# Decay attention with a gated MLP on one core: softmax divided behind the value product by reciprocals sent through DRAM, the convolution off TensorE, decays of two pairs on it, and a new order

## The chip, the cores and the metric

One core of one Trainium2 chip. The metric is device time of one execution in microseconds (us). Times of the kernel before: 525.26 us, the median of 3 runs (524.59 to 526.09).

## The reference

```
scores = q @ k^T / sqrt(D)                      # q, k, v: (8, 8, 576, 64), f: (8, 8, 576)
cum    = cumsum(log(clip(f, 1e-4, 1)))
scores = where(j > i, -1e9, scores + cum[i] - cum[j])
attn   = exp(scores - max(scores));  attn = attn / (sum(attn) + 1e-9)
x      = (attn @ v) as (8, 576, 512)            # heads side by side
gate   = sigmoid(sum over k < 5 of conv_w[k] * x[s - 4 + k])    # by channel, causal
out    = (gate * (x @ w_val)) @ w_out
```

## The kernel before

The 64 heads go two at a time: 32 pairs, four pairs to a batch. A pair's 64 + 64 channels fill the 128 partitions. Its queries go in four blocks of 128 (block j against 128(j+1) keys, causal) for each head, and the last 64 queries of both heads together, 128 rows against all 576 keys: nine score blocks a pair, in three groups u = 0, 1, 2 (`SG`). For each pair:

- `load_pair`, `load_rest`: SP loads q and k (`Xr`), v (`vt`), and by broadcast reads from the DRAM tensor `decd` the decays of its two heads (`dm`, 640 KB each, `dl`, 144 KB each); POOL masks the diagonal (`affine_select`, L317).
- `plan_t`, `plan_s`: products in PSUM (`banks`), for pairs 0 to 3 in f32, then in three f32r products of high and low parts. DVE adds the decays and takes the row's minimum of the negated scores (`red`, L465), ACT takes the exponential with its sum (`ex`, L469; `P`, `Pl`, sums in `zs`). `rec` (L478, L479) adds 1e-9 and takes reciprocals, in two halves of a pair. `norm` (`times`, L276 on ACT, L278 on POOL and DVE) multiplies each exponential block by its column of `rz`.
- `plan_pt`: TensorE (PE) transposes the normalized blocks (L510, L528, L529), ACT or DVE copies them to SBUF (`pt`).
- `plan_pv`: value products in two halves of queries, copied to `x32` (`X`, ACT or DVE, L271). The convolution over x is one first tap and four multiply-adds on DVE (`cv`, L612); for pairs 0 and 1 (`NCV = 2`) it is five matmuls a half on PE against diagonal matrices. ACT takes the tanh (sigmoid in disguise, `half_tanh`, L586), with its table set loaded at pair 0.
- `plan_moe`: for each batch, x @ w_val (`Mv`), gated on DVE (`H`), and the product with w_out (`Mo`), all as three f32r products.

Pair 0's decays are not read from DRAM: PE adds them as products of a selecting matrix `pick` with the table `st` in SBUF (`SD`, `decays`), ahead of the score products, in the same banks. The weights arrive as 64-bit numbers and are decoded on ACT, DVE and POOL in the first 100 us (`decode`).

The order of the work is written out: `TABLE` is a list of steps, each with its engine and PSUM bank, and `Plan.order` records the instructions in it. Each engine runs its own in that order and waits where it must. SP issues all loads, in order too. The helper `mm` (L256) records the matmuls, `copy` (L271) the copies, `load` (L283) the DMAs.

Of the kernel before, what the change touches and what calls it, by code (L numbers as in the profile page):

```python
# [7 lines left out]
F32 = mybir.dt.float32  # L8
# [17 lines left out]
NCV = 2  # L26
# [7 lines left out]
XZ, XK4, XK, XW = 512, 640, 704, 1216  # L34
XP = ((0, XK4), (XK4, XW))
# [17 lines left out]
6y18A27Z28b2af36A19f26M028x28y18h38s078i36B18R48e18c18d38k018-
3a348o058l18t28p16C3ai38q038r28m018z19j29l28g12329k19g1aj3ad39h294073545v29929m16N0952a549i19q29y39x3by19a16J006K09b29618n26L29729c16D18u058v12416E2aD
06aE26O2bp49v19818D019w18B048C1ak00352bw3bx38E2aF1bn49d29u39r1au0149G076P1dq46U066F26G29z39H1ae36R07bz3al2am18H1az2ap2aq1252an29A00aA19B26Q36S09t1ao19
I056V09s39E009J17003710av2aB2bj4bt39K05ar2aw1ax26T2ay19F1bv3as1bT006W28I2at29M0276X16Y2aJ3aC16Z06aG2bU2aM35w18X4bl4aP39P19O29Q29N19L17229C04dw46-
0aI16H2ds4bV1aU02aV18J28K29D1aL1dy4dE3dH1bu39R079S1aK1bA052306_2bB2dF1bH2bK014bF2aO1bC1eO4bL2732bG19T06bR2bI19U1aN3aY07bS1bP2bQ1aZ28L2aH3a-
03a_1bD2b0065b42b317d00b216I1aQ07bM1eG4bN2dI27803790eX3eY3dG3aS05bE1bO1du4e001aR1bJ2bX1b12ab4bZ2c807e12g04c91eV17506eM4aW04aT1b-
37437607a2aX1e21c407dD3g24dT0542729V1c517728F2dJ02613262br47b1bW2dC3dU2eI4283d-
2c22c01b707dQ2dR19X1dK2b503dL1fW4dW28G3c31ce02dM2fY4dO2dP17c37e0dY2dZ1bY3b62c12dN1c603b81b_37i06cc079Y2eK49Z2b91dS2bb17f19W27g47j0eW2c71d_1e52cf1cd17n  # L60
019-
2ha4dX19_2ba2e41e72cg074cj2eU37o0ch2dV17k1ca00ck1e32e93eb3bc2ci28M1fg02fh2bd2gb1cb1be2fi1ef05hi4e62cn07eS37p1g91cl03e81eZ02401cm17q4dA4eT3co2cp2f7063c
r3eg1ea3e-
2f22hg4f31e_1gc3ed05f02f42fe2f11fa2ho3a017s07eh00f51ee2ei1cq37l47t07u1el02cA04fb1ec2ej01cB0hr1ek1f82ff1g63cs2cx05cy0bf2f62em1bg1ep023cC2ct2er1cI04fm1f
# [115 lines left out]
def tile_decay_attention_gated_mlp(  # L180
# [224 lines left out]
    def plan_s(i):  # L405
# [7 lines left out]
        for u, group in enumerate(SG):  # L413
# [59 lines left out]
            if u == 1:  # L473
                continue
# [337 lines left out]
```

## Time and profile before

| | us |
|---|---|
| median of 3 runs | 525.26 |
| the profiled execution | 527.36 |
| its span | 525.6 |
| PE busy (4412 matmuls) | 510.6, 97% |
| DVE busy | 450.2, 86% |
| ACT busy | 410.1, 78% |
| POOL busy | 292.1, 56% |
| DMA (16 engines) busy, mean | 54.0% of the span, 94.62 MB |

Busy time counts an engine's instructions, not what they wait for. PE's matmuls are pipelined, so their durations overlap: what one step costs is read from the start of one to the start of the next. The span is the profiled execution's own program; a sum of changes is made against its 527.36 us.

### The profile page before, as it was taken

How to read it: one execution, taken by the hardware profiler on the slowest of the kernel's cores; microseconds unless marked ns; L12 is line 12 of the kernel's file. 1: busy time of each engine (PE TensorE's matmuls, PEld its weight loads, DVE VectorE, ACT ScalarE, POOL GpSimd, SP SyncE). 2: the span in 40 equal slices, each digit the busy share in tenths (PEclk: the TensorE clock that was granted, in tenths of full speed). 3: DMA queues.
4: the chain of work that ended last, by engine and by line, in shares of the span. 5: the costliest groups of instructions: out<-in, count | busy, mean ns of one | idle time of the engine just before them, and what ended most of it. 6: DMA issues, size and time to landing. Idle time of an engine off the chain costs nothing.

```text
span 525.6 us, 12791 instructions
## 1 busy us (share of the span) xinstructions
PE 510.6 (97%) x4412; PEld 448.0 (85%) x4412; DVE 450.2 (86%) x1257; ACT 410.1 (78%) x1121; POOL 292.1 (56%) x408
## 2 busy tenths in 40 slices
PE   6899999999999999999999999999999999999997
PEld 4567779988999889998899888899899988898995
DVE  6998999989879888998988998988899998866771
ACT  4999999988868897777979978899988777464221
POOL 3636679674666674667795748653645554324100
PEclk9999999999999999999999999999999999999999
DMA  7988675656265736546736556666577271500012
GB/s 257 305 292 289 216 217 196 183 166 238 87 233 179 256 123 221 181 155 250 245 134 211 195 185 226 215 214 192 183 217 225 78 236 69 186 27 1 21 60 101
DMA packets 29905, 95.44 MB, mean 182 GB/s; under 512 B 3920, under 2 KB 3920, under 8 KB 29840
## 3 DMA queue, kind: packets, MB, share of 16 engines
q1 hardware_dynamic: 29840, 94.62, 54.0%
q8 instruction: 35, 0.57, 0.5%
q14 instruction: 30, 0.25, 0.1%
HBM read 84.69 MB, written 9.91 MB: 180 GB/s over the span
## 4 chain that ended last, share of the span: by engine, by line
PE 79%; ACT 9%; DVE 5%; DMA 3%; issue 2%; SPq 1%; POOL 0%; DVEq 0%; ACTq 0%
PE banks L256 64%; PE banks L510 12%; ACT P L469 3%; PE banks L528 2%; DMA Xr<-in_x_dram 2%; DVE banks L465 2%; ACT P L276 1%; ACT pt L271 1%; DMA dm<-decd 1%; SPq L283 1%; DMA Pl<-in_f_dram 1%; PE banks L529 1%; ACT Xh L271 0%; ACT gate L701 0%; ACT x L271 0%
## 5 line engine op out<-in xcount | busy, mean ns | idle before, releaser
L469 ACT ACTIVATE P<-banks,negm 128x128 f32<-128x128 f32 (+3 forms) x256 | 134.2, 535 | 22.0 <-DVE negm L465 20.7
L278 POOL TENSOR_SCALAR P<-P,rz 128x128 f32<-128x128 f32 (+3 forms) x113 | 77.4, 691 | 98.0 <-DVE rz L479 69.4
L465 DVE CUSTOM_DVE_ANT_0 banks<-banks,dm 128x128 f32<-128x128 f32 (+3 forms) x256 | 120.0, 513 | 11.5 <-PE banks L256 4.5
L256 PE MATMUL banks<-xh,wall 128*128 128x288 f32 x512 | 120.2, 306 | 0.0
L612 DVE SCALAR_TENSOR_TENSOR gate<-x,cw,gate 128x576 f32<-128x576 f32 x120 | 104.9, 879 | 1.3
L510 PE MATMUL banks<-ident,P 128*128 128x128 f32 x640 | 99.2, 276 | 4.2 <-ACT P L276 1.2
L271 ACT COPY pt<-banks 128x512 f32<-128x512 f32 (+2 forms) x206 | 84.5, 444 | 22.4 <-PE banks L510 10.7
L256 PE MATMUL banks<-pt,vt 128*64 128x128 f32 (+2 forms) x1408 | 95.6, 290 | 0.3 <-DVE pt L271 0.3
L256 PE MATMUL banks<-wall,hh 128*128 128x512 f32 x288 | 93.3, 405 | 0.0
L256 PEld LDWEIGHTS banks<-pt,vt 128*64 128x64 f32 x1408 | 83.6, 137 | 11.2 <-issue 2.4
L510 PEld LDWEIGHTS banks<-ident,P 128*128 128x128 f32 x640 | 75.4, 140 | 16.5 <-POOL P L278 1.8
L256 PEld LDWEIGHTS banks<-xh,wall 128*128 128x128 f32 x512 | 86.3, 188 | 0.7
L256 PE MATMUL banks<-xl,wall 128*128 128x288 f32 x256 | 75.4, 294 | 0.0
L317 POOL TENSOR_SCALAR_AFFINE_SELECT dm<-dm 128x256 f32<-128x256 f32 x126 | 56.7, 475 | 29.4 <-DMA dm<-decd 21.8
L271 DVE COPY pt<-banks 128x512 f32<-128x512 f32 (+2 forms) x114 | 49.3, 450 | 17.1 <-PE banks L510 10.4
L276 ACT ACTIVATE P<-P,rz 128x256 f32<-128x256 f32 (+3 forms) x100 | 58.2, 597 | 5.9 <-DVE rz L479 5.8
L256 PE MATMUL banks<-Xh 128*128 128x288 f32 (+4 forms) x280 | 57.6, 340 | 0.4 <-ACT P L469 0.4
L256 PEld LDWEIGHTS banks<-wall,hh 128*128 128x128 f32 x288 | 50.2, 189 | 7.7 <-ACT P L469 0.2
L256 PE MATMUL banks<-wall,hl 128*128 128x512 f32 x144 | 56.7, 394 | 0.0
L469 ACT ACTIVATION_READ_ACCUMULATOR P<-banks,negm 128x1 f32 x256 | 53.5, 209 | 0.0
L256 PE MATMUL banks<-Xh,Xl 128*128 128x288 f32 (+4 forms) x280 | 52.9, 313 | 0.0
L256 PE MATMUL banks<-Xl,Xh 128*128 128x288 f32 (+4 forms) x280 | 52.9, 313 | 0.0
(109 smaller groups left out, 875.3 us busy)
## 6 DMA issues: line engine op xcount, KB each, us to landing
dm<-decd SPq DMA_DIRECT2D x62, 640.0 KB, 5.3
Xr<-in_x_dram SPq DMA_DIRECT2D x32, 608.0 KB, 5.6
vt<-in_v_dram SPq DMA_DIRECT2D x32, 320.0 KB, 4.9
out_dram<-ot SPq DMA_DIRECT2D x36, 256.0 KB, 3.3
dl<-decd SPq DMA_DIRECT2D x62, 144.0 KB, 4.7
ot<-in_w_val_dram SPq DMA_DIRECT2D x2, 512.0 KB, 5.4
wu<-in_w_val_dram SPq DMA_DIRECT2D x2, 512.0 KB, 6.2
ot<-in_w_out_dram SPq DMA_DIRECT2D x2, 512.0 KB, 5.0
```

Of the source, the lines that this page charges most:

```text
L256: nc.tensor.matmul(out, lhsT=lhsT, rhs=rhs, start=start, stop=stop)
L271: (eng.copy if eng is nc.scalar else eng.tensor_copy)(out=out, in_=in_)
L276: eng.activation(out=out, in_=in_, func=AF.Copy, scale=col)
L278: eng.tensor_scalar(out=out, in0=in_, scalar1=col, scalar2=0.0, op0=ALU.mult, op1=ALU.add)
L283: lambda e: (nc.sync if e == "SP" else nc.scalar).dma_start(out=out, in_=in_), reads, writes, **kw)
L317: nc.gpsimd.affine_select(out=t, in_=t, pattern=[[0, 2], [-1, P]], base=0, channel_multiplier=1, compare_op=ALU.is_ge, fill=-BIG)
L465: nc.vector.tensor_tensor_reduce(out=sl, in0=sl, in1=add[:, o:o + ext], op0=ALU.add, op1=ALU.min, scale=-0.125, scalar=3.0e38, accum_out=n ...
L469: nc.scalar.activation(out=dst[:, o:o + ext], in_=bank(key)[:, c0:c0 + ext], func=AF.Exp, bias=negm[r][:, col], scale=-1.0, accum_out=zs[r ...
L510: nc.tensor.transpose(out=bank(key)[:, c:c + P], in_=Pt[m][:, BOFF[b] + P * j:BOFF[b] + P * j + P], identity=ident)
L528: nc.tensor.transpose(out=bank(key)[:, P * j:P * j + P], in_=Pl[r][:, D + P * j:D + P * j + P], identity=ident)
L529: nc.tensor.transpose(out=bank(key4)[0:D, 0:P], in_=Pl[r][:, 0:D], identity=ident)
L612: eng.scalar_tensor_tensor(out=gt, in0=src, scalar=wt_, in1=gt, op0=ALU.mult, op1=ALU.add)
```

## The change

- The exponentials go to PE undivided. The reciprocals of a pair's nine sums are computed at once, into nine extra columns of `Pl`, and transposed with its last piece, so that they come out as nine rows; a copy brings them to `rt`, two DMAs write them to the DRAM tensor `rzd`, and two DMAs read them back, each row broadcast to 64 partitions, into the pair's `x32`. The copy of a value product to `x32` becomes a multiplication by what lies there, on DVE alone. `x32` has three buffers (`NXR`).
- `NCV = 0`: the convolutions of pairs 0 and 1 go to DVE like the others.
- `ND = 2`: decays of pairs 0 and 1 are added by PE, in groups u = 0 and 2 behind the score products, in u = 1 ahead of them. Their loads from `decd` fall away.
- The tanh's table set, which has the exponential too, is loaded behind the logarithm at the start. Other keys' order in `Xr`, other buffers for the start's scratch.
- A new `TABLE`, for other costs of the steps.

```diff
-NCV = 2
+NCV = 0
+ND = 2
+NXR = 3
...
 TABLE = """
-0040b20x30930240C40a20E10430520c20y30F20s010H20G20d10e20630t000I10J20f20N40K20Y40g20L20j20M20k20l20740h10i10P10Q20S20R20T10u000U20W10r003k42940m43a42d
...
+0240040430s010w000c20u040e20f10740g10v030b30F40t010Q40520h20H10i20932g001240k12i00K20n20l10m10z32r0570C33342e30j10o43540I20J20E32h00q40630L10B32n22o12
...
-    Pl = tiles(NQ, [P, S], F32, "Pl")
+    Pl = tiles(NQ, [P, S + NN], F32, "Pl")
...
+    rt = tiles(NQ, [D + NN, P], F32, "rt")
+    rzd = dram.tile([NP, 2, S], F32, name="rzd")
...
-        for h in range(2 if i else 0):
+        for h in range(2 if i >= ND else 0):
             m = (2 * i + h) % NH
...
+    act("st0", 1.3, z, lambda: nc.scalar.preload_act_table_set(EXP_TANH), [("ln",)], [("act",)])
...
+            added = {}
+            if deep and u != 1:
+                for q, pair in enumerate(pairs if u == 0 else ((0,),)):
...
+                    pe("SD", e * 4 / 2400.0 + 0.03, p + 0.004 + 0.002 * q, lambda pair=pair, decays=decays: decays(pair, False),
...
+        def rec():
+            rz = Pl[r][:, S:]
+            nc.vector.tensor_scalar(out=rz, in0=zs[r], scalar1=1e-9, scalar2=None, op0=ALU.add)
+            nc.vector.reciprocal(out=rz, in_=rz)
...
-            def norm(eng, sl=sl, c=4 * u + n):
-                times(eng, sl, sl, rz[r][:, c:c + 1])
...
+            nc.tensor.transpose(out=bank(key4)[0:D + NN, 0:P], in_=Pl[r][:, L0:], identity=ident)
...
+        any_("PE", {"ACT": 0.16, "DVE": 0.21}, p + 0.02, lambda eng: copy(eng, rt[r][D:], bank(key4)[D:D + NN, 0:P]), [key4], [("rt", r)])
+        load("rzw", 0.1, p + 0.03, rzd[i, :, 0:L0].rearrange("h (j q) -> h j q", q=P), rt[r][D:D + 2 * NB], [("rt", r)], [("rzd", i, 0)])
+        load("rzw", 0.1, p + 0.03, rzd[i, :, L0:], rt[r][D + 2 * NB:], [("rt", r)], [("rzd", i, 1)])
+        for h in range(2):
+            load("rzr", 0.65, p + 0.04, x32[i % NXR][D * h:D * h + D, T0:], rzd[i, h:h + 1].to_broadcast([D, S]),
+                 [("rzd", i, 0), ("rzd", i, 1)], [("xb", i % NXR, h)])
...
-            def ev(eng, key=key, qa=qa, qb=qb):
-                copy(eng, xr[:, T0 + qa:T0 + qb], bank(key)[:, 0:qb - qa])
-            any_("X", ap(qb - qa), p, ev, [key], [("x", r, half)])
+            def ev(key=key, qa=qa, qb=qb):
+                o = xr[:, T0 + qa:T0 + qb]
+                nc.vector.tensor_tensor(out=o, in0=bank(key)[:, 0:qb - qa], in1=o, op=ALU.mult)
+            dve("X", (qb - qa) / 960.0 + 0.075, p, ev, [key, ("xb", rx, 0), ("xb", rx, 1)], [("x", rx, half)])
```

Three places of the order, before and now. First, PE in the start: `gate0,dm0` are the decays of pair 0, `Xr0` its products, `ident` alone the products that keep PE going, `P0` the transposition of a block of P. Before (two decays of 512 stand just ahead):

```order
L256 MATMUL banks_125<-gate0_109,dm0_68 128x256 x2
L256 MATMUL banks_125<-Xr0_73 128x512 x2
L256 MATMUL banks_125<-Xr0_73 128x256 x2
L256 MATMUL banks_125<-gate0_109,dm0_68 128x384 x2
L256 MATMUL banks_125<-Xr0_73 128x384 x2
L256 MATMUL banks_125<-gate0_109,dm0_68 128x128 x2
L256 MATMUL banks_125<-Xr0_73 128x128 x2
L256 MATMUL banks_125<-gate0_109,dm0_68 128x288
L256 MATMUL banks_125<-Xr0_73 128x288
L256 MATMUL banks_125<-gate0_109,dm0_68 128x288
L256 MATMUL banks_125<-Xr0_73 128x288
L510 MATMUL banks_125<-ident_64,P0_79 128x128 x2
```

Now:

```order
L371 MATMUL banks_126<-ident_64 128x128 x20
L253 MATMUL banks_126<-Xr0_73 128x512 x2
L253 MATMUL banks_126<-Xr0_73 128x256 x2
L253 MATMUL banks_126<-gate0_111,dm0_68 128x256 x2
L253 MATMUL banks_126<-gate0_111,dm0_68 128x384 x2
L253 MATMUL banks_126<-Xr0_73 128x384 x2
L253 MATMUL banks_126<-gate0_111,dm0_68 128x128 x2
L253 MATMUL banks_126<-Xr0_73 128x128 x2
L253 MATMUL banks_126<-gate0_111,dm0_68 128x512 x2
L511 MATMUL banks_126<-ident_64,P0_79 128x128 x2
L253 MATMUL banks_126<-Xr0_73 128x288 x2
L253 MATMUL banks_126<-gate0_111,dm0_68 128x288 x2
```

The first products of Xr stand ahead of the decays and a first transposition ahead of the last 64 queries (the rows of 288).

Second, SP in the middle of the program: before, a stretch of loads, and now the loads about pair 11 (`rt1`, `x322`) and pair 12 (`rt0`). Before:

```order
L283 DMA dm0_68<-decd_67 128x1280
L283 DMA Xr0_73<-in_x_dram 128x1216
L283 DMA dm2_70<-decd_67 128x1280
L283 DMA dm1_69<-decd_67 128x1280
L283 DMA out_0_dram<-ot_121 128x512
L283 DMA Xr1_74<-in_x_dram 128x1216
L283 DMA dl1_72<-decd_67 64x576
L283 DMA out_0_dram<-ot_121 128x512
```

Now:

```order
L280 DMA dm1_69<-decd_67 128x1280
L280 DMA x321_94<-rzd_98 64x576
L280 DMA rzd_98<-rt0_96 2x4x128
L280 DMA rzd_98<-rt0_96 2x1x64
L280 DMA x322_95<-rzd_98 64x576 x2
L280 DMA dm2_70<-decd_67 128x1280
L280 DMA Xr0_73<-in_x_dram 128x1216
L280 DMA dm1_69<-decd_67 128x1280
L280 DMA dm0_68<-decd_67 128x1280
L280 DMA vt1_88<-in_v_dram 128x640
L280 DMA rzd_98<-rt1_97 2x4x128
L280 DMA dm2_70<-decd_67 128x1280
```

Of pair 11 the two reads follow on the two writes they wait for, with the loads of later pairs behind them; of pair 12 three other loads stand between its two writes.

Third, the evacuation of a value product. Before, on ACT, two copies of one pair (`x320`) among the others:

```order
L271 COPY pt2_86<-banks_125 128x512
L271 COPY pt0_84<-banks_125 128x256
L271 COPY x320_95<-banks_125 128x384
L271 COPY x320_95<-banks_125 128x192
L276 ACTIVATE gate0_109<-x320_95,cw_66 128x576
L271 COPY pt0_84<-banks_125 128x512
L469 ACTIVATE Pl0_82,zs0_91<-banks_125,negm0_89 128x576
```

Now, on DVE, pair 11 (`x322`). Ahead of this piece stand the copy of pair 11 to `rt1` and an `xl`; the rows of L479 with a bank are row minima of later pairs:

```order
L479 ISA banks_126,negm0_89<-banks_126,dm1_69 128x512
L479 ISA negm0_89 128x1
L268 CAST xh4_103<-x321_94 128x576
L616 SCALAR_TENSOR_TENSOR gate0_111<-x321_94,cw_66,gate0_111 128x576 x2
L479 ISA banks_126,negm1_90<-banks_126,dl1_72 128x576
L479 ISA negm1_90 128x1
L490 TENSOR_SCALAR Pl0_82<-zs0_91 128x9
L491 RECIPROCAL Pl0_82<-Pl0_82 128x9
L587 TENSOR_TENSOR xl4_109<-x321_94,xh4_103 128x576
L268 COPY pt0_84<-banks_126 128x512
L580 TENSOR_TENSOR x322_95<-banks_126,x322_95 128x384
L580 TENSOR_TENSOR x322_95<-banks_126,x322_95 128x192
```

The two multiplications wait for the reads into `x322`; behind them come the gate's first tap, the next pair's copy to `rt0`, and further minima.

## Rows read from the trace of the kernel before

**Rows 1.** Busy time of each engine in six stretches of the span: start:end, length, then busy us and (instructions) of PE, its weight loads, DVE, ACT and POOL, the granted share of TensorE's clock, the DMA engines' mean busy share and GB/s.

```profile
0.00:17.59 17.59, 12.33 (x56) 8.29 (x56) 13.21 (x43) 9.72 (x23) 5.97 (x24) 1.00 0.75 242
17.59:80.00 62.41, 57.85 (x471) 44.11 (x471) 58.44 (x172) 60.62 (x169) 40.38 (x59) 1.00 0.78 263
80.00:200.00 120.00, 119.36 (x1087) 107.60 (x1086) 105.98 (x296) 103.23 (x283) 81.03 (x104) 1.00 0.57 190
200.00:320.00 120.00, 119.77 (x1091) 107.69 (x1089) 109.03 (x312) 99.31 (x280) 80.63 (x105) 1.00 0.58 196
320.00:440.00 120.00, 119.35 (x1094) 107.24 (x1095) 107.22 (x310) 102.67 (x285) 65.86 (x99) 1.00 0.60 194
440.00:525.60 85.60, 81.89 (x618) 73.08 (x616) 56.30 (x130) 34.50 (x86) 18.21 (x20) 1.00 0.18 61
```

**Rows 2.** TensorE's timeline, 31 to 34 us (start, busy us, instructions of one form merged, idle time before in brackets): the convolution of one half of pair 0 and what follows it.

```profile
31.13 0.65 PE L256 MATMUL banks<-x,h 128*128 128x288 f32 x2
...
33.56 0.65 PE L528 MATMUL banks<-ident,Pl 128*128 128x128 f32 x4
```

**Rows 3.** TensorE's timeline from the first decays to the first transposition of P, and one later piece of the same products for pair 2.

```profile
7.76 2.93 PE L256 MATMUL banks<-gate,dm 64*128 64x512 f32 x8 [1.41 <-DVE gate L361]
10.48 2.07 PE L256 MATMUL banks<-Xr 64*128 64x512 f32 x8
12.39 0.81 PE L256 MATMUL banks<-gate,dm 64*128 64x384 f32 x4
13.03 0.81 PE L256 MATMUL banks<-Xr 64*128 64x384 f32 x4
13.68 0.38 PE L256 MATMUL banks<-gate,dm 64*128 64x128 f32 x4
13.90 0.39 PE L256 MATMUL banks<-Xr 64*128 64x128 f32 x4
14.21 0.75 PE L256 MATMUL banks<-gate,dm 128*128 128x288 f32 x2
14.80 0.65 PE L256 MATMUL banks<-Xr 128*128 128x288 f32 x2
15.29 0.65 PE L256 MATMUL banks<-gate,dm 128*128 128x288 f32 x2
15.77 0.65 PE L256 MATMUL banks<-Xr 128*128 128x288 f32 x2
17.59 0.44 PE L510 MATMUL banks<-ident,P 128*128 128x128 f32 x2 [1.17 <-ACT P L276]
...
34.25 1.56 PE L256 MATMUL banks<-Xr 64*128 64x512 f32 x8
```

**Rows 4.** The timeline of all engines in the start: two DMA issues, TensorE's wait for Xr, the first cuts of the table on ACT, the first full reciprocal; and, from the view of the tile Xr in the first 20 us, its loads' time to landing.

```profile
2.04 0.58 SPq L283 DMA_DIRECT2D u<-in_conv_w_dram  x1
...
3.61 0.43 SPq L283 DMA_DIRECT2D Xr<-in_x_dram  x1
...
7.22 1.01 ACT L359 ACTIVATE gate<-x,ref 128x256 f32<-128x256 f32 x2 [1.43 <-DVE ref L352]
...
10.34 0.51 PEld L256 LDWEIGHTS banks<-Xr 64*128 64x128 f32 x4 [0.38 <-DMA Xr<-in_x_dram]
...
16.39 0.18 DVE L479 RECIPROCAL rz<-rz 128x4 f32<-128x4 f32 x1
...
DMA to landing us min/median/max: 4.8/6.2/6.7
```

**Rows 5.** Who made TensorE wait: waiter, releaser, us in total, times, longest.

```profile
PE banks L256 <- ACT P L469: 1.3, 3, 0.6
PE banks L510 <- ACT P L276: 1.2, 1, 1.2
PE banks L510 <- DVE P L278: 1.1, 2, 0.6
PE banks L510 <- POOL P L278: 0.7, 2, 0.5
PE banks L256 <- ACT gate L586: 0.7, 1, 0.7
```

**Rows 6.** DMA issues of the whole span (count, KB each, median us from issue to landing), and SP's issue of two dl loads in its timeline.

```profile
dl<-decd SPq DMA_DIRECT2D x62, 144.0 KB, 4.7
decd<-gate SPq DMA_DIRECT2D x1, 116.0 KB, 3.5
u<-in_conv_w_dram SPq DMA_DIRECT2D x1, 20.0 KB, 2.4
...
12.29 1.10 SPq L283 DMA_DIRECT2D dl<-decd  x2
```

**Rows 7.** Groups of instructions by line and form (count, busy us in all, mean ns of one, idle time before): the multiply-add of the gate, a row minimum, an xl, all on DVE; then the normalization on POOL and on ACT, from the page.

```profile
L612 DVE SCALAR_TENSOR_TENSOR gate<-x,cw,gate 128x576 f32<-128x576 f32 x120 | 104.9, 879 | 1.3
L465 DVE CUSTOM_DVE_ANT_0 banks<-banks,dm 128x512 f32<-128x512 f32 x64 | 45.2, 715 | 1.6 <-PE banks L256 1.6
L579 DVE TENSOR_TENSOR xl<-x,xh 128x576 fp32r<-128x576 f32 x13 | 9.8, 755 | 0.0
...
L278 POOL TENSOR_SCALAR P<-P,rz 128x128 f32<-128x128 f32 (+3 forms) x113 | 77.4, 691 | 98.0 <-DVE rz L479 69.4
L276 ACT ACTIVATE P<-P,rz 128x256 f32<-128x256 f32 (+3 forms) x100 | 58.2, 597 | 5.9 <-DVE rz L479 5.8
```

More of the change, by code (lines that the diff above doesn't have):

```diff
@@ L291, in tile_decay_attention_gated_mlp @@
     st = gate[0].rearrange("p g s -> p (g s)")[:, 0:SW + S]
[L292 to L294 removed]
+    ft, cum, ones = Pl[1][:, 0:S], x32[1][:, T0:], vt[1].rearrange("p a h d -> p (a h d)")[:, 0:S]
+    pick = [dm[2 * n][:, 0:2 * P] for n in range(ND)]
+    kf, kc, ko = [("Pl", 1)], [("xb", 1, 0), ("xb", 1, 1)], [("vt", 1)]
     kst = [("gate", 0, g) for g in range(G)]
@@ L381, in tile_decay_attention_gated_mlp @@
     pool("start", 0.8, z + 0.3, mk_tri, (), [("tri",)])
-    for r in range(NQ):
+    for r in range(NXR):
         pool("start", 0.1, z + 0.4 + r, lambda r=r: nc.gpsimd.memset(x32[r][:, 0:T0], 0.0), (), [("xpad", r)])
@@ L420, in plan_s, with decays, go @@
             pairs = ((0, 1), (2, 3))
-            def decays(group=group, keys=keys, pairs=pairs):
-                for n in [n for pair in pairs for n in pair]:
+            deep = i < ND
+            def decays(pair, start, group=group, keys=keys, u=u):
+                if u == 2:
+                    for a, e in ((0, 288), (288, 576)):
+                        mm(bank(keys[0])[:, 224 + a:224 + e], pick[i][:, P:], st[:, SW + a:SW + e], False, True)
+                    return
+                for n in pair:
                     h, j, c0 = group[n]
                     hs = slice(D * h, D * h + D)
-                    mm(bank(keys[n])[:, c0:c0 + EXT[j]], pick[hs, 0:P], st[hs, BOFF[j]:BOFF[j] + EXT[j]], True, False)
-            if i == 0 and u == 0:
-                pe("SD", 2.0, p - 0.15, decays, [("dm", 0), *ktab[:2], *kst], list(dict.fromkeys(keys.values())),
-                   cols=3072, mode=1)
-            def go(group=group, keys=keys, u=u, pairs=pairs, decays=decays):
+                    mm(bank(keys[n])[:, c0:c0 + EXT[j]], pick[i][hs, 0:P], st[hs, BOFF[j]:BOFF[j] + EXT[j]], start, not start)
+            def go(group=group, keys=keys, u=u, decays=decays):
                 if u == 2:
@@ L743, in tile_decay_attention_gated_mlp, with scores @@
     plan_w("wo", w_out, woh, wol, 3.6)
-    for i in range(NP):
+    def scores(i):
         if i:
@@ L749, in tile_decay_attention_gated_mlp @@
         plan_s(i)
+    for i in range(NP):
+        if i == 0 or i >= ND:
+            scores(i)
         plan_pt(i)
+        for n in range(1, ND if i == 0 else 0):
+            scores(n)
         plan_pv(i)
```

283 lines of the change are left out of this document (131 added, 152 removed).

## Prediction

> **What bounds the kernel now.** I read the busy time by stretch first, then TensorE's timeline, then its waits. In the busy times by stretch [rows 1] the reader is to see TensorE (PE) at 358.5 of the 360 us between 80 and 440 us, while DVE stands at 322.2, ACT at 305.2 and POOL at 227.5 there. What PE does not fill lies at the ends: 5.3 us idle before 17.59, 4.6 us from there to 80, and 3.7 us in the last stretch, behind the last product. So from 80 us on, work taken from PE comes off the time and work taken from another engine does not. From 17.59 to 80 all three are close: ACT 60.6, DVE 58.4, PE 57.9 of 62.4. The granted clock is 1.00 in every stretch, so no term is a clock term. The profiled execution took 527.36 us; the median of the runs is 525.26, 2.1 lower. I make the sum against the first and carry it to the second.
>
> **The convolution leaves PE.** A half's ten matmul instructions start at 31.13, and the next step's start at 33.56 [rows 2]: 2.43 us. Two pairs by two halves are 4 x 2.43 = 9.7 us of PE gone. The eight multiply-adds that replace them go to DVE at 879 ns each [rows 7], 7.0 us. Behind 80 us that is free, since DVE has 37.8 us idle in 360. Ahead of 80 us DVE has 4.0 idle in all, but the gates of pairs 0 and 1 are not wanted before the first batch's value product. I cost it at nothing, and take up the other case below.
>
> **Decays of pair 1 on PE.** Pair 1 now pays what pair 0 paid. The blocks of 384 take 0.64 us (12.39 to 13.03), those of 128 0.22 (13.68 to 13.90), the last 64 queries 0.59 and 0.48 (14.21 to 14.80, 15.29 to 15.77) [rows 3]. Those of 512 and 256 lie between 1.56 us, which the same shapes of Xr take at 34.25, and 2.72, which they took at 7.76 with a wait in it; I take 1.5, near the unstalled row. Together 3.4 us (to 4.6). **PE's work: -9.7 + 3.4 = -6.3 us** (-5.1 to -6.5). Its transposes, value products and projections stay as they are.
>
> **The start.** Before, PE waits for the first cut of the decays (7.76), then for Xr (10.34), and the first transposition starts at 17.59, when ACT has divided a block by a reciprocal of 16.39 [rows 3, 4]. In the new order the first products need no decays, Xr is issued where conv_w was, at 2.04 and not 3.61, and the transposition needs only the exponential. Xr's loads take 4.8 to 6.7 us to land, so products start between 6.8 and 8.7. The tables come off ACT from 7.22 on at about 0.5 us each, ahead of their use. Then PE has 1.56 us of products (as at 34.25), 1.5 of their decays, and 1.8 for the blocks of 384 and 128 with theirs (12.39 to 14.21), and a transposition starts at 11.7 to 13.6. The last 64 queries, done by 16.4 before, are then still to come (2.1 us), so the same work stands done at 13.8 to 15.7 and not at 17.7: a gain of 2.0 to 3.9. It needs ACT and DVE to keep up, which do nearly the same operations there, less two reciprocals. **I take -3**, between -1 and -3.9.
>
> **Division behind the value product.** The old normalization takes 77.4 us of POOL, 58.2 of ACT [rows 7] and some of DVE, all beside PE. PE waited for it in four places that the waits show: 1.2 us on ACT's (the start, counted above), 1.1 on DVE's, 0.7 on POOL's, and 0.7 on the gate of the convolution [rows 5]. The last three, 2.5 us, go; late next is the exponential just ahead, for which PE already waits 1.3 in three places. **I take -1.3**, half, between 0 and -2.5. The evacuation of a value product, on ACT mostly, becomes a DVE multiplication, which takes part of what DVE sheds.
>
> **The road through DRAM.** New, per pair: a copy of nine rows to rt, two small writes, two reads of 144 KB (the shape of dl, 4.7 us to landing), then the multiplication on DVE. SP takes 0.55 us for each issue. A write of 116 KB took 3.5 us to land [rows 6]; the small one can't be shown by a row, and a 20 KB read of the start at 2.4 is the nearest shorter one [rows 6]. So issue, write, issue, read are 0.55 + 3.5 + 0.55 + 4.7 = 9.3 us by the nearest rows. The Trainium skill (DMA: Bandwidth & Descriptors, Anatomy of one DMA) puts a DMA at about 2.0 us plus its bytes at 436 GB/s, measured there on the gpsimd path: by that the pair of transfers would be 4.3 us, and no multiplication would wait. No trace here shows a landing of 2.0, so the sum goes by the rows.
>
> What waits: DVE is in order, so behind the multiplication stand the row minima of the next pair, the exponentials after them and, last, PE's transpositions. In the order of pair 11 (shown above) DVE has between the copy and the multiplication two xl (755 ns), a minimum of 512 (715), two multiply-adds (879) and five smaller operations: 4.0 us for the named ones and about 6 with the rest. There it waits some 3 us. Fourteen of the 32 pairs have their reads right behind the writes in SP's queue; the others have other loads between, and a later place of use. Fourteen times 3 is 42 us of DVE waits against DVE's 37.8 idle us: PE, which works off products of another batch meanwhile, loses **0**, with +4 as the other end of what I still call this case. The added 9.2 MB, less 1.6 of pair 1's decays, raise a DMA share of 0.58 by some 0.04.
>
> **Sum.** -6.3 - 3 - 1.3 = -10.6: 527.36 becomes 516.8 for a profiled execution, and the median 525.26 becomes **514.7 us**. Its bounds are -6.5 - 3.9 - 2.5 = -12.9 and -5.1 - 1 + 4 = -2.1, so 512 to 523.
>
> **Rivals.**
> *SP's queue and DVE stall on the road through DRAM (slower).* In those 14 pairs SP stands for the write's landing, and the next pair's decay and Xr loads stand behind it; DVE stands in front of the multiplication. With 5 us for each (a write of 3.5 and a read of 4.7 behind a full queue, nothing hidden by DVE) it is 70 us, 32 above DVE's idle time: 514.7 + 32 = 547. It decides from (37.8 + 10.6)/14 = 3.5 us of DVE wait in each of them. For it: DVE's 89% between 80 and 440. Against: ACT and POOL are relieved, three x buffers in place of two, and PE has work of other batches at hand.
> *The stretch to 80 us stays with DVE.* The 7.0 us of multiply-adds come into a stretch with 4.0 idle; PE loses the 3 us that don't fit and the 1.3: 519.
> *The waits of that stretch go.* ACT, its busiest engine, sheds the normalizations and most evacuations; if PE's idle 4.6 us there go altogether, in place of my 1.3, the start gives 3.9, and the products that stand in busy time but stretched by late operands (2.72 us for 1.5 at 7.76 is one) save another 2, it is 514.7 - 3.3 - 0.9 - 2 = 508.5.
>
> **How the numbers follow.** The sum's case has 0.50, the DRAM stall 0.13, the DVE stretch 0.17, the vanished waits 0.20. The measurement tells 0.3% (1.6 us) from no change. All but the stall are faster by more, save a part of the first case that a stall of a few us for PE would take past 523.7: faster 0.83, same 0.04, slower 0.13. The range of 505 to 524 leaves out the stall and a little below 508.5.
>
> **What would show it.** Right: no PE matmul on x and u; PE busy near 504; PE idle under 2 us between 80 and 440; the first transposition of P at 11 to 13 us; no PE wait on the division. Multiplications on DVE that wait for x<-rzd are to be seen, 0 to 4 us each, with PE still full. Wrong: PE idle or stretched in the steady stretch, released by a row minimum or an exponential whose DVE stood before a multiplication; loads of dm that are issued late behind a rzd read on SP; a first transposition at 15 us or later.

## Result and profile after

The changed kernel took **529.42 us** (median of 17 runs, 526.74 to 533.64) against 526.09 us (17 runs, 524.59 to 527.49) for the kernel before on the same chip: ratio 1.0075, 95% interval 1.0051 to 1.0098. That is 0.75% slower, where 514.7 us and faster had been predicted; it lies outside the range as well. The profiled execution took 527.19 us (span 525.3), near the low end of its runs, and that of the kernel before 527.36 us, near the high end of its own: the two traces stand side by side without the loss that the medians show.

Busy time by stretch in the changed kernel, columns as in [rows 1]:

```profile
0.00:17.59 17.59, 14.96 (x92) 10.99 (x94) 12.78 (x41) 13.05 (x33) 8.69 (x29) 1.00 0.75 233
17.59:80.00 62.41, 54.11 (x499) 42.63 (x497) 57.56 (x170) 58.16 (x164) 34.53 (x44) 1.00 0.89 286
80.00:200.00 120.00, 118.56 (x1074) 107.78 (x1072) 104.29 (x285) 85.35 (x248) 56.62 (x69) 1.00 0.64 210
200.00:320.00 120.00, 117.35 (x1051) 104.43 (x1047) 102.52 (x277) 81.82 (x241) 56.77 (x70) 1.00 0.66 213
320.00:440.00 120.00, 119.29 (x1109) 106.45 (x1111) 106.59 (x296) 81.89 (x245) 56.20 (x71) 1.00 0.62 201
440.00:525.30 85.30, 80.27 (x583) 71.31 (x579) 54.92 (x120) 27.36 (x64) 11.53 (x12) 1.00 0.22 77
```

The columns of PE add up to 504.5 us, the 504 that was predicted. ACT and POOL are relieved by 56 and 58 us between 80 and 440 (305.2 to 249.1, 227.5 to 169.6). But PE idles more. Against [rows 1] its idle time is 2.6 us less ahead of 17.59, 3.7 us more from there to 80 (8.3 for 4.6), 3.3 us more between 80 and 440 (4.8, where under 2 was predicted) and 1.3 us more behind that: 5.7 us for 6.1 us less work, so the two spans are nearly the same.

The largest of these stands ahead of 80 us, in the stretch that the work was taken from. From 40 to 80 us ACT is full in the changed kernel and PE is not (before, then changed, columns as in [rows 1]):

```profile
40.00:80.00 40.00, 37.11 (x329) 29.96 (x328) 37.70 (x111) 38.59 (x108) 28.34 (x37) 1.00 0.72 231
```

```profile
40.00:80.00 40.00, 35.85 (x359) 29.77 (x357) 37.91 (x112) 39.62 (x112) 26.75 (x31) 1.00 0.92 295
```

TensorE's timeline of the start, to be held against [rows 3]:

```profile
7.08 1.56 PE L253 MATMUL banks<-Xr 64*128 64x512 f32 x8 [1.21 <-DMA Xr<-in_x_dram]
...
10.64 1.03 PE L253 MATMUL banks<-gate,dm 64*128 64x512 f32 x4
11.60 0.44 PE L511 MATMUL banks<-ident,P 128*128 128x128 f32 x2
...
12.84 1.13 PE L253 MATMUL banks<-gate,dm 128*128 128x288 f32 x4
13.81 0.38 PE L511 MATMUL banks<-ident,P 128*128 128x128 f32 x2
```

The first transposition starts at 11.60 and the last 64 queries are done by 13.81: the early ends of what was predicted (11.7 to 13.6, and 13.8 to 15.7). The start's gain is there. How the lead goes is seen from one instruction that both kernels have, the start of each batch's last value projection on PE (us, read from the timelines of the two kernels and of the one without the road, below):

| batch | 0 | 1 | 2 | 3 | 4 | 5 | 6 | 7 |
|---|---|---|---|---|---|---|---|---|
| before | 113.3 | 162.2 | 228.7 | 290.9 | 365.0 | 425.6 | 475.5 | 508.0 |
| changed, less before | -10.9 | -4.7 | -3.5 | -2.6 | -3.9 | -1.9 | -2.8 | +1.2 |
| no road, less before | -9.1 | -2.9 | -2.4 | -1.8 | -5.5 | -4.0 | -5.9 | -3.4 |

The 10.9 us at batch 0 are not the whole sum come true. The new order brings that step forward: from there to batch 1 the changed kernel makes 480 matmuls and the kernel before 440, and PE's idle time explains only 1.4 of the 6.2 us lost between the two columns. By work and idle time (6.1 us less work, 10.9 us of idle time ahead of 80 us for 9.8 before) the lead at 80 us is, as an estimate, some 5 us, half of what the sum said. From batch 1 on the changed kernel gives it back in small pieces. Each row is one execution: the traces of e10, e16 and e17 (below), which are the kernel before up to some 280 us, reach batch 0 1.3 to 2.4 us earlier than the row of the kernel before.

Who waited, in the changed kernel (us in total, times, longest): POOL's masks and ACT's exponentials, DVE's multiplication; then SP and PE.

```profile
POOL dm L314 <- DMA dm<-decd: 66.9, 23, 14.0
...
ACT P L483 <- DVE negm L479: 35.5, 39, 3.3
ACT Pl L483 <- DVE negm L479: 30.9, 16, 4.2
...
DVE x L580 <- DMA x<-rzd: 8.3, 7, 4.4
```

```profile
SPq L280 <- DVE negm L479: 75.4, 32, 8.0
SPq L280 <- DMA rzd<-rt: 35.1, 29, 4.9
SPq L280 <- ACT rt L268: 31.1, 7, 15.1
```

```profile
PE banks L253 <- ACT P L483: 3.5, 3, 1.9
PE banks L511 <- ACT pt L268: 2.5, 3, 1.1
PE banks L511 <- ACT P L483: 2.1, 3, 1.2
...
PE banks L253 <- ACT Pl L483: 1.7, 2, 1.4
PE banks L253 <- DVE x L580: 1.4, 4, 0.5
```

DVE's own wait on the road is small, 8.3 us, where the prediction had 42. But POOL's wait for dm is 66.9, for 21.8 before (the row below), and SP stands 35.1 us for the writes' landing.

```profile
POOL dm L317 <- DMA dm<-decd: 21.8, 17, 4.2
```

PE waits 7.3 us for exponentials, against 1.3 in [rows 5]. Of these 7.3 us, 4.7 lie between 17.59 and 80 us, the 2.1 of L511 and, of the 3.5 of L253, the row below; so do the 2.5 us for copies of pt.

```profile
PE banks L253 <- ACT P L483: 2.6, 2, 1.9
```

One later case in the timeline of all engines: DVE stands until the store of an earlier ot has landed, so a row minimum behind it, the exponential behind that and PE's next scores are late:

```profile
319.10 0.69 DVE L691 TENSOR_SCALAR ot<-banks 128x512 f32<-128x512 f32 x1 [3.13 <-DMA out_dram<-ot]
...
320.06 0.76 DVE L479 CUSTOM_DVE_ANT_0 banks<-banks,dl 128x576 f32<-128x576 f32 x1
...
320.92 0.74 ACT L483 ACTIVATE Pl<-banks,negm 128x576 f32<-128x576 f32 x1 [4.16 <-DVE negm L479]
...
321.80 0.44 PE L253 MATMUL banks<-Xh 64*128 64x384 f32 x2 [0.27 <-ACT Pl L483]
```

The road itself is plain at the last pair, in the chain of waits (start, us, what):

```profile
483.45 0.27 ACT rt L268
483.73 0.60 SPq L280
484.33 0.05 issue
484.38 1.70 DMA rzd<-rt
486.16 0.50 SPq L280
486.67 0.05 issue
486.72 2.90 DMA x<-rzd
489.74 0.10 DVE x L580
```

From copy to multiplication 6.0 us with nothing in the way; the median of the 32 pairs is 11.2 us (from the timelines of rt and x). The prediction's 9.3 us for issue, write, issue, read lies between.

### The profile page after: what moved, and what is told of

It is laid out like the page before. It is cut to its first block, busy times and chain, and to the rows that moved or that the text cites. A ratio compares the mean times of both kernels' runs of the same rounds, so it can differ in the third digit from the quotient of the medians.

```text
span 525.3 us, 12611 instructions
## 1 busy us (share of the span) xinstructions
PE 504.5 (96%) x4392; PEld 443.6 (84%) x4392; DVE 438.7 (84%) x1186; ACT 347.6 (66%) x991; POOL 224.3 (43%) x293
## 5 line engine op out<-in xcount | busy, mean ns | idle before, releaser
L479 DVE CUSTOM_DVE_ANT_0 banks<-banks,dm 128x384 f32<-128x384 f32 (+3 forms) x256 | 120.5, 512 | 10.1 <-PE banks L253 6.6
L268 ACT COPY pt<-banks 128x256 f32<-128x256 f32 (+2 forms) x235 | 94.5, 437 | 41.7 <-PE banks L511 22.7
L253 PE MATMUL banks<-xh,wall 128*128 128x288 f32 x512 | 113.2, 300 | 0.0
L616 DVE SCALAR_TENSOR_TENSOR gate<-x,cw,gate 128x576 f32<-128x576 f32 x128 | 108.9, 857 | 1.1
L253 PE MATMUL banks<-pt,vt 128*64 128x128 f32 (+2 forms) x1408 | 95.8, 290 | 1.9 <-ACT P L483 1.9
L253 PEld LDWEIGHTS banks<-pt,vt 128*64 128x64 f32 x1408 | 84.0, 137 | 13.8 <-ACT P L483 3.1
L511 PE MATMUL banks<-ident,P 128*128 128x128 f32 x640 | 89.0, 277 | 5.5 <-ACT pt L268 2.5
L253 PE MATMUL banks<-wall,hh 128*128 128x512 f32 x288 | 91.9, 400 | 2.0 <-ACT P L483 0.9
L314 POOL TENSOR_SCALAR_AFFINE_SELECT dm<-dm 128x256 f32<-128x256 f32 x122 | 57.6, 498 | 84.0 <-DMA dm<-decd 66.9
L253 PEld LDWEIGHTS banks<-xh,wall 128*128 128x128 f32 x512 | 85.0, 188 | 1.3 <-DVE h L648 0.3
L511 PEld LDWEIGHTS banks<-ident,P 128*128 128x128 f32 x640 | 71.1, 140 | 15.3 <-ACT P L483 4.0
L253 PE MATMUL banks<-xl,wall 128*128 128x288 f32 x256 | 75.4, 295 | 0.0
L397 POOL TENSOR_TENSOR Xl<-Xr,Xh 128x576 fp32r<-128x576 f32 (+1 forms) x41 | 63.0, 1545 | 19.9 <-ACT Xh L268 16.0
L253 PE MATMUL banks<-Xh 128*128 128x288 f32 (+4 forms) x280 | 59.2, 339 | 3.7 <-ACT Pl L483 1.7
L253 PEld LDWEIGHTS banks<-wall,hh 128*128 128x128 f32 x288 | 51.2, 188 | 11.7 <-DVE x L580 1.4
L253 PE MATMUL banks<-wall,hl 128*128 128x512 f32 x144 | 56.4, 391 | 0.0
L253 PE MATMUL banks<-Xh,Xl 128*128 128x288 f32 (+4 forms) x280 | 54.8, 315 | 0.1
L253 PE MATMUL banks<-Xl,Xh 128*128 128x288 f32 (+4 forms) x280 | 54.0, 313 | 0.0
L253 PEld LDWEIGHTS banks<-xl,wall 128*128 128x128 f32 x256 | 48.2, 188 | 0.5
L587 POOL TENSOR_TENSOR xl<-x,xh 128x576 fp32r<-128x576 f32 x20 | 29.2, 1462 | 44.7 <-ACT xh L268 41.0
```

Source lines behind the costliest of these rows:

```text
L253: nc.tensor.matmul(out, lhsT=lhsT, rhs=rhs, start=start, stop=stop)
L268: (eng.copy if eng is nc.scalar else eng.tensor_copy)(out=out, in_=in_)
L314: nc.gpsimd.affine_select(out=t, in_=t, pattern=[[0, 2], [-1, P]], base=0, channel_multiplier=1, compare_op=ALU.is_ge, fill=-BIG)
L397: eng.tensor_tensor(out=Xl[r][:, a:e], in0=Xr[r][:, a:e], in1=Xh[r][:, a:e].bitcast(F32), op=ALU.subtract)
L479: nc.vector.tensor_tensor_reduce(out=sl, in0=sl, in1=add[:, o:o + ext], op0=ALU.add, op1=ALU.min, scale=-0.125, scalar=3.0e38, accum_out=n ...
L511: nc.tensor.transpose(out=bank(key)[:, c:c + P], in_=Pt[m][:, BOFF[b] + P * j:BOFF[b] + P * j + P], identity=ident)
```

## Experiments

Theory 1: the road through DRAM makes the new idle time. Theory 2: the new order makes it, whatever the DMAs do. All runs stand beside runs of the kernel before (medians 526.16 to 526.54).

| run | median us | ratio to before (95%) |
|---|---|---|
| e1_no_road | 522.54 | 0.9937 (0.9916 to 0.9957) |
| e2_road_unused | 526.03 | 0.9994 (0.9973 to 1.0014) |
| e3_reads_twice | 549.23 | 1.0437 (1.0396 to 1.0478) |
| e14_tiny_behind | 528.04 | 1.0026 (1.0007 to 1.0046) |
| e15_tiny_ahead | 533.24 | 1.0113 (1.0085 to 1.0142) |
| e13_closed_road | 549.96 | 1.0453 (1.0414 to 1.0491) |
| e5_one_read | 642.04 | 1.2170 (1.2131 to 1.2208) |
| e6_one_read_act_writes | 668.20 | 1.2680 (1.2638 to 1.2723) |
| e9_road_on_pool | 616.45 | 1.1698 (1.1662 to 1.1734) |
| e4_before_one_tap | 527.04 | 1.0014 (1.0001 to 1.0027) |
| e10_before_late_scores | 525.79 | 0.9984 (0.9970 to 0.9998) |
| e16_before_fewer_taps | 526.14 | 0.9994 (0.9982 to 1.0006) |
| e17_before_fewer_taps_scores | 524.31 | 0.9962 (0.9950 to 0.9975) |
| e7_before_no_norm | 525.83 | 0.9984 (0.9964 to 1.0004) |
| e8_before_no_norm_one_tap | 525.73 | 0.9990 (0.9975 to 1.0004) |
| e11_scores_twice | 532.26 | 1.0110 (1.0082 to 1.0138) |
| e12_no_road_late_scores | 520.37 | 0.9873 (0.9844 to 0.9902) |

### What the road costs

**e1_no_road.**

```diff
+ load(..., skip=i >= 8)          # rzw and rzr: nothing is issued
- in1=o
+ in1=o if i < 8 else one_.to_broadcast([P, qb - qa])
```

> The changed kernel, but from pair 8 on the two writes to rzd and the two reads from it are not issued, and the multiplication takes a column of ones in place of what they bring (so the output of batches 2 to 7 is left undivided); same places in the order, same number of DVE instructions. Theory 1 (the road through DRAM makes PE's new idle time between 150 and 515 us, where the lead of some 8 us is lost): with it gone the lead stays, 519 to 523, and PE idle between 80 and 440 falls from about 5 us to 2. Theory 2 (the new order itself: exponentials that come late behind DVE and ACT in order, whatever the DMAs do): within 1.5 us of the changed kernel's 529.4.

522.54: 6.9 us below the changed kernel, as theory 1 said. Busy time between 80 and 440:

```profile
80.00:200.00 120.00, 118.14 (x1056) 106.77 (x1052) 105.46 (x286) 85.20 (x247) 55.75 (x70) 1.00 0.64 204
200.00:320.00 120.00, 118.69 (x1085) 106.26 (x1086) 104.47 (x282) 83.50 (x245) 59.27 (x73) 1.00 0.58 193
320.00:440.00 120.00, 120.00 (x1124) 107.47 (x1121) 105.61 (x296) 82.68 (x248) 54.25 (x69) 1.00 0.55 182
```

PE's idle time falls to 3.2 us, not to 2. Ahead of 80 us, where the road is still there, PE idles 10.7 us, like the changed kernel (10.9). And 522.5 is still 7.8 above the prediction: the road is half of the error.

**e2_road_unused.**

```diff
- x32[i % NXR][D * h:D * h + D, T0:]
+ (x32[i % NXR][D * h:D * h + D, T0:] if i < 8 else wu[1].bitcast(F32)[D * h:D * h + D, 0:S])
```

> The changed kernel, but from pair 8 on the two reads from rzd land in a buffer that nobody reads, and the multiplication takes a column of ones (output of batches 2 to 7 left undivided). SP's waits and the traffic stay, DVE's wait for the landing goes. If of theory 1 DVE's standing in front of the multiplication is the part that costs (in the changed kernel 8.3 us of waits, longest 4.4): as without the road, 519 to 523. If SP's standing (loads of dm and x late behind it) or the traffic is: as the changed kernel, 528 to 530. Theory 2: 528 to 530 as well.

526.03, between the two: of 6.9 us, 3.4 are the multiplication's standing and 3.5 what the road does to SP and the DMA engines. The halves are rough: counted in the kept traces from the place where the runs begin to differ (138 us, the first read of pair 8), e1 gains 6.3 us and e2 4.6. Nor is all of POOL's wait for dm the road's: it is 39.3 us in e1, 58.7 in e2 and 66.9 in the changed kernel.

**e3_reads_twice.**

```diff
+ if twice is not None:
+     nc.sync.dma_start(out=twice, in_=in_)
```

> The changed kernel, but from pair 8 on each read from rzd is issued a second time right behind itself, into a buffer that nobody reads: two more issues of 0.5 us on SP for a pair and 7 MB more. Theory 1 with SP or the traffic as its part: 531 to 537. Theory 1 with DVE's wait as its part: 529 to 532, since only the second read's landing is delayed by an issue. Theory 2: 529 to 530.

+19.8, more than twice the most that was expected. DVE's wait for x<-rzd rises from 8.3 to 15.2 us, POOL's for dm from 66.9 to 92.0, PE's for x from 1.4 to 8.0:

```profile
POOL dm L319 <- DMA dm<-decd: 92.0, 22, 21.0
...
DVE x L585 <- DMA x<-rzd: 15.2, 6, 5.6
...
PE banks L253 <- DVE x L585: 8.0, 7, 3.1
```

**e14_tiny_behind, e15_tiny_ahead.** The same SP time without the bytes.

```diff
+ for n in range(2):      # behind the second read, or ahead of the first
+     nc.sync.dma_start(out=wu[1].bitcast(F32)[D * n:D * n + 1, 0:D], in_=rzd[i, n:n + 1, 0:D])
```

> The changed kernel, from pair 8 on with two reads of 256 bytes from rzd, into a buffer that nobody reads, issued behind the pair's second read: 1 us of SP for a pair, next to no bytes, and the road itself not longer. If the 20 us of the run with reads made twice were SP's time in front of the loads: 540 to 550. If they were the second read, which stood later by an issue, or the bytes: 529 to 533.

> As the run before it in this set, but the two reads of 256 bytes stand ahead of the pair's first read: the same 1 us of SP for a pair, and the road longer by 1 us. If the road's length is what counts: well above the run with them behind, 545 to 555. If SP's time alone counts: the same as that run.

Behind the reads 1 us of SP for a pair costs nothing (528.04, even 1.4 below the changed kernel); ahead of them it costs 3.8 us, 5.2 more than behind. So SP's issues as such are free. That the longer road costs these 3.8 us is not shown: in its trace e15 is 5.5 us behind the changed kernel's trace at 131 us already, ahead of its first changed read, and loses 1.7 us more from there to the end. In any case 533 is far less than the 545 to 555 expected. What is left of the 20 us of the reads made twice lies in their bytes, or in the second read's landing; those two are not told apart.

**e13_closed_road.**

```diff
+ for n, e, _ in [x for x in rows if self.nodes[x[0]]["cls"] == "rzr"]:
+     ...     # each rzr moves to right behind the last step that it depends on
```

> The changed kernel, with the order on SP changed alone: the two reads of a pair are issued right behind the later of its writes, ahead of the loads that stood between them (in 18 pairs something stood there). SP then stands for the write's landing in every pair, and the loads come some 2 us later; the road gets shorter by 0.5 to 5 us in those pairs. If the time from the copy of the nine rows to the multiplication is what the kernel pays for (read twice: +0.5 us of it at the median, +20 us of time): faster than the changed kernel, 522 to 527. If SP's standing in front of the loads is: 530 to 540.

+20.5, as the other side said: with SP standing for the landing in front of the loads, POOL waits 88.4 us for dm, and PE for exponentials:

```profile
POOL dm L319 <- DMA dm<-decd: 88.4, 23, 15.2
...
PE banks L516 <- ACT P L488: 11.1, 7, 3.7
```

Two things weaken this. The road did not get shorter, as was meant: from copy to multiplication it takes 12.3 us at the median, for 11.2. And most of the loss is early: at 103 us of the changed kernel's trace e13 is 16.8 us behind, of 26.4 at the end, and 9.6 of the 11.1 us of PE's wait lie in its first 103 us. That loads put into the road lengthen it, and reads put ahead of loads make those late, fits e3 and e13; they do not price the two apart.

**e5_one_read, e6_one_read_act_writes, e9_road_on_pool.** Three ways to take the road off SP, meant as improvements.

```diff
- for h in range(2): load("rzr", ..., x32[i % NXR][D * h:D * h + D, T0:], rzd[i, h:h + 1].to_broadcast([D, S]), ...)
+ load("rzr", ..., x32[i % NXR][:, T0:], rzd[i][:, None, :].to_broadcast([2, D, S]), ...)   # e5, e6: issued once
+ q = nc.scalar if cls == "rzw" else nc.sync                                                # e6
+ q = nc.gpsimd if cls in ("rzw", "rzr") else nc.sync                                       # e9, two reads
```

> The changed kernel, with the two reads of a pair (64 partitions each) made one read of 128 partitions at the place of the second: the same bytes, the same waits, 32 issues of some 0.5 us fewer on SP. If SP's time is what the road costs (48 more issues of 0.5 us cost 20 us in the run with the reads made twice): 519 to 525, up to the 522.5 of the run without the road or a little below, since pairs 0 to 7 gain too. If traffic was what cost there: 528 to 530.

> As the run with one read, and the two writes of a pair are issued from ACT's queue, at the place that they had against ACT's own work. SP sheds another 64 issues of 0.63 us and its wait for the copy of the nine rows. If SP's time is what the road costs: 516 to 522. If ACT's issues and its waits for a copy that DVE made come in front of exponentials that PE waits for: slower than with one read alone, by 1 to 5.

> The changed kernel with the four small DMAs of a pair (two writes to rzd, two reads) issued from POOL's queue at the places that they had on SP's against POOL's own work. SP is rid of the road: its loads no longer stand behind it. DVE's wait for the landing stays. If SP's standing costs what the two runs without and with an unused road differ by (526.0 - 522.5 = 3.5): about 526, less a little for pairs 0 to 7. If POOL, which now stands for the writes' landing, makes xl and the masks of dm late: 530 or more.

All three fail, by 87 to 139 us. The one read moves the same bytes but lands late. At the last pair it is issued at 595.50, and DVE waits 8.55 us:

```profile
595.50 0.51 SPq L286 DMA_DIRECT2D x<-rzd  x1
603.26 0.56 DVE L589 TENSOR_TENSOR x<-banks,x 128x384 f32<-128x384 f32 x1 [8.55 <-DMA x<-rzd]
```

In the trace's packets, the 128 rows of that read are moved from 596.79 to 602.83 with 2.0 in flight at a time; the two reads of the changed kernel's last pair take from 487.46 to 489.19 with 8.2 in flight. The Trainium skill (DMA: Bandwidth & Descriptors, Why a DMA increments its semaphore by 16 and not by 1) says that a DMA runs on the largest number of engines up to 16 that divides the slowest dimension of both its patterns; here that dimension is the two heads, so two engines, and the trace agrees. So e5 tests something else than meant: a road 4.6 us longer (15.8 us from copy to multiplication at the median, 11.2 before the edit) costs 113 us, 3.5 a pair. DVE waits 96.8 us for the reads and PE 36.9 for the multiplications behind them. PE idles 50 us between 80 and 440, and its granted clock falls, which adds to it:

```profile
80.00:200.00 120.00, 100.17 (x856) 90.80 (x855) 86.22 (x234) 72.28 (x206) 51.83 (x61) 0.93 0.55 172
```

From ACT's queue the writes cost 26 us more (e6 against e5). On POOL's (e9) the writes stood 79.0 us, mostly for the copies, the reads 49.5 for the writes' landing, and DVE waited 48.9 us for the reads.

### What PE's work is worth

**e4_before_one_tap, e10_before_late_scores.** PE's work taken out of the kernel before, early and late.

```diff
  for t in range(KC):                       # e4
+     if t == 0:
          mm(bank(key)[:, 0:e - a], dv[t], xr[:, t + a:t + e], True, True)
+ if 20 <= i < 24:                          # e10
+     prods = prods[:1]
```

> The kernel before, but of the five products of each half of the convolution on PE only the first is made (the gates of pairs 0 and 1 leave out four taps). This takes 4 x 2.43 x 4/5 = 7.8 us of PE's work ahead of 80 us and nothing else. If PE's work is what bounds the time from there on, as the prediction took it: 526.1 - 7.8 = 518.3 (517 to 520). If a saving in that stretch is lost to DVE's and ACT's chains later on, as in the changed kernel: 522 to 526.

> The kernel before, with one of the three products of the scores of pairs 20 to 23 (the two corrections are left out, so these scores are less exact): PE sheds 4 x 1.76 = 7.1 us between some 310 and 390 us, where it is busy all the time. If PE's work bounds the time there, as the prediction read it: 526.2 - 7.1 = 519 (518 to 520.5). If work taken from PE is worth as little there as ahead of 80 us (one tap: nothing): 524.5 to 526.5.

Next to nothing: +0.9 for 7.8 us less, and -0.4 for 7.1 us less where PE was busy all the time. The windows show where the 7.1 went; the kernel before, then e10, 300 to 360 us:

```profile
300.00:320.00 20.00, 19.93 (x164) 17.32 (x163) 18.74 (x51) 15.72 (x48) 11.07 (x17) 1.00 0.61 200
320.00:340.00 20.00, 19.69 (x172) 17.10 (x173) 17.42 (x53) 17.75 (x48) 13.84 (x19) 1.00 0.70 230
340.00:360.00 20.00, 20.00 (x207) 18.72 (x206) 18.56 (x53) 18.85 (x57) 10.21 (x16) 1.00 0.61 197
```

```profile
300.00:320.00 20.00, 18.90 (x145) 15.82 (x143) 19.45 (x55) 17.19 (x53) 13.65 (x19) 1.00 0.68 219
320.00:340.00 20.00, 17.24 (x139) 14.17 (x141) 18.39 (x53) 17.80 (x52) 12.94 (x17) 1.00 0.67 221
340.00:360.00 20.00, 20.00 (x195) 18.62 (x192) 15.74 (x45) 16.43 (x47) 7.22 (x14) 0.91 0.61 187
```

Between 300 and 340 PE idles 3.5 us more: it is there earlier, and others are not. Its longest waits in e10 from 288 to 366 us (L278 is the normalization, of which the prediction had said that it stands beside PE):

```profile
PE banks L512 <- POOL P L278: 1.9, 2, 1.7
PE banks L256 <- DVE pt L271: 0.9, 1, 0.9
```

Behind that the granted clock is 0.91 for 20 us, which takes 1.8 more: 5.3 of the 7.1 us. That the span is 1.6 shorter is no gain of the edit: at the last value projection of batch 3, ahead of the first product left out, e10 is 2.4 us ahead already. From there to the end it takes 0.8 us longer, so some 2.6 us of the saving are not accounted for. In e4 it is the same ahead of 80 us:

```profile
17.59:80.00 62.41, 53.69 (x432) 40.20 (x431) 57.46 (x171) 59.60 (x167) 39.38 (x59) 0.92 0.78 258
```

PE is busy 4.2 us less there than in [rows 1], ACT is still at 59.6 of 62.4, and the clock is 0.92 and not 1.00, worth 4 to 5 us.

**e16_before_fewer_taps, e17_before_fewer_taps_scores.**

```diff
+ if not 18 <= i < 24:                      # both; e17 has e10's edit too
      eng.scalar_tensor_tensor(out=gt, in0=src, scalar=wt_, in1=gt, op0=ALU.mult, op1=ALU.add)
```

> The kernel before, with the four multiply-adds of the convolution left out for pairs 18 to 23 (24 x 0.87 = 21 us of DVE's work gone between some 280 and 390 us; the gates of these pairs have one tap). PE's work is whole. If PE bounds this stretch: 525 to 526.5, nothing gained. If DVE does: 505 to 515.

> As the run before it in this set, and one of the three products of the scores of pairs 20 to 23, 7.1 us of PE's work, which gave 0.4 us alone. If PE and DVE hold the stretch together (each catches up only where the other lets it): 518 to 520, the 7.1 us come out once DVE is relieved. If the saving goes elsewhere (the clock that falls after PE's idle, the exponentials on ACT): within 1.5 of the run with fewer taps alone.

21 us less on DVE alone give nothing either. Both cuts together give 1.8 us beyond that, where PE's cut alone had given 0.4: DVE holds part of it, and 5 of the 7.1 us still do not come out. Here the clock stays at 1.00; PE idles 2.4 us from 300 to 340 while ACT is busy 36.4 of 40; the longest wait in it, 1.1 us, is for the normalization on POOL again.

**e7_before_no_norm, e8_before_no_norm_one_tap.**

```diff
  def norm(eng, sl=sl, c=4 * u + n):
-     times(eng, sl, sl, rz[r][:, c:c + 1])
+     pass
```

> The kernel before, but the normalization of the exponentials is left out on every engine (output undivided); reciprocals, evacuations, the convolution on PE and the order stay. The prediction's own term: -1.3 (0 to -2.5), so 523.6 to 526.1. If ACT's time, full ahead of 80 us, is what bounds that stretch: PE's idle 4.6 us and the stretched products there go, -5 to -8, 518 to 521.

> Both edits of the kernel before: no normalization, and one of the five products of each half of the convolution on PE. One tap alone gave no gain (527.0 against 526.2). If ACT's time stood behind that, PE's 7.8 us count once ACT is relieved: 5 to 8 below the run without normalization. If they count for nothing whatever ACT does (the clock, DVE, or a later limit takes them): within 1.5 of it.

-0.5 for the whole normalization, within the interval of no change, and -0.6 with PE's 7.8 us taken out too. So ACT was not what hid those 7.8 us, or not alone. In the trace of e8 the granted clock from 17.59 to 80 us is 0.92, where it is 1.00 in e7, and PE idles 7.9 us there for 3.1: the clock and waits take it, as in e4.

**e11_scores_twice, e12_no_road_late_scores.** The price of PE's work in the new order.

```diff
+ if i in (2, 3):                           # e11
+     go = (lambda g: lambda: (g(), g()))(go)
+ if 20 <= i < 24:                          # e12, on e1
+     prods = prods[:1]
```

> The changed kernel, with the scores of pairs 2 and 3 made twice (the second time over the first, same result): 2 x 3.4 = 6.9 us more of PE ahead of 80 us. If PE's work counts there in the new order: 535 to 537. If that stretch belongs to ACT and DVE, or its lead is lost later in any case: 528 to 531.

> The run without the road, and in it one of the three products of the scores of pairs 20 to 23 (7.1 us of PE's work gone, as in the kernel before). If PE bounds the steady stretch of the new order once the road is out of it: 522.5 - 7.1 = 515.4 (514.5 to 517). If the exponentials' and row minima's chain does: 520 to 523.

6.9 us more early cost 2.8 (0.4 of it), and 7.1 us less late, with the road gone, give 2.2 (0.3 of it): more than in the old order, but neither end of what was expected. It is the fastest run, but it leaves out the division and two products; no version with all of the work beat the kernel before.

## Why the prediction was wrong

- **PE's work, -6.3.** Its size held (PE 510.6 to 504.5), its worth did not. The step that failed is the first reading, "from 80 us on, work taken from PE comes off the time". The work itself goes ahead of 80 us, where the prediction had all three engines close and still counted the whole term: there PE's idle time rose by 3.7 us, behind an ACT that is busy 39.6 of the last 40. The rival "the stretch to 80 us stays with DVE" described this, with DVE in ACT's place; the rival by which the waits of that stretch go had the sign wrong. Taken out alone, PE's work gave +0.9 and -0.4 us in the old order, and 0.3 to 0.4 of itself in the new. [Rows 1] gave a hint: PE busy 358.5 of 360 us, but its weight loads 322.5 (107.60 + 107.69 + 107.24), 90%, no more than DVE's 322.2. The Trainium skill (Perfetto Trace Analysis, Identifying the Most-Contended Engine) says that the busy share of matmuls is no good measure of TensorE's headroom, and to go by that of weight loads (and by the arithmetic done against the peak) instead. By the weight loads PE had 10% to spare; e10, where 7.1 us less work gave 0.4, agrees that PE was not the bound, but no run shows that the 10% can be filled.
- **The start, -3.** Right in mechanism and time (transposition at 11.60, last queries done at 13.81). With the normalization it would make up what the run without the road gains, 522.5 against 526.2, -3.6; the two were not taken apart on the chip.
- **Division, -1.3.** -0.5 (e7), inside the bounds. The four waits of [rows 5] went, and others of the same kind took their place.
- **The road, 0, with +4 as the other end.** The second step that failed: "PE, which works off products of another batch meanwhile, loses 0". It costs 6.9 us from pair 8 on. The landing times were taken long (1.7 and 2.9 us at the last pair, for 3.5 and 4.7), and DVE's waits are only 8.3 us for the 42 feared. The Trainium skill (DMA: Bandwidth & Descriptors, Anatomy of one DMA), by whose figure 4.3 us is the estimate for the pair of transfers, was nearer: the trace has 4.6. But from it the prediction concluded that no multiplication would wait, and at the last pair one waited 4.4 us. What was missed is the part that is no wait of the multiplication, 1.7 to 3.5 us: SP, standing for copy and landing, makes loads of dm late (66.9 us of POOL's waits, 39.3 without the road from pair 8 on), and behind dm stand minima and exponentials. That this part is SP's standing and not the added bytes is argued, not shown: e13 speaks for it with the 9.6 us that it loses behind 103 us, and e3 leaves the bytes a part.
- **The rival that was slower** had both mechanisms and the wrong price: 547 for a kernel at 529. The same road a little worse stands at 549 to 550 (e3, e13), so what decides it is small.
- **The sum.** -6.3 became 0, -4.3 became -3.6, 0 became +6.9: 3.3 above before, which is what was measured. This adds medians from different kernels, so it is bookkeeping, not proof that the parts add. The road is half of the error; the other half, 7.8 us, is there without it.

What stays open: why 21 us of DVE, 7 us of PE or the whole normalization each give nothing in the kernel before. One engine's work is not it. The waits of e10 and e17 point to the chain of minimum, exponential, normalization (on POOL), transposition and copy, whose steps wait for each other in an order written for their old times, but no run relieved that chain as a whole, or took the normalization and late products out together.

## What to carry to other kernels

A share of 99% busy matmuls beside 85 to 90% on ACT and DVE was no bound here: before a cut of work enters a sum, take the same amount out of the old kernel, and see what it is worth. A round trip through DRAM is priced also by what stands behind it on the issuing queue, not only by who waits for its data. Where two traces are compared behind an edit, see first how far apart they were ahead of it: here up to 5.5 us. In an order fixed by hand, a saving on one engine is worth what the next engine's step lets through.

## What was not expected of the hardware

- One broadcast read of 288 KB with the two heads as its outer dimension moved with 2.0 packets in flight and 6.0 us of moving; two reads of 144 KB with 64 rows outermost took 1.7 us for both.
- The granted clock can fall behind small gaps of PE: 0.91 over 20 us behind 2.8 us of idle time in the 20 us ahead of it, the longest gap 1.7 us (e10); 0.92 ahead of 80 us with four fifths of the convolution out (e4); 0.93 in e5. It does not always: it stayed at 1.00 behind 2.1 us of idle time in the same 20 us, the longest gap 1.1 us (e17). Work taken from PE was in part paid back in this way.
- The changed kernel spreads over 7 us from run to run, the kernel before over 3. Much of it can arise early: the traces of e1, e2, e3, e14 and e15, which do the same work as the changed kernel up to pair 8, stand 1.0 to 5.5 us behind it at 103 us.
